# One core, two independent layers in one program: from a hand-written interleaving to a dependency graph with its own static list scheduler

## The chip, the core and the metric

The kernel runs on one core of a Trainium2 chip. The metric is the device time of one execution in microseconds (us), as the median of three runs. The engines, as the profile names them: PE (matrix multiply, with its weight loads shown apart as PEld), DVE and ACT (both can read PSUM, where PE writes), POOL (works on SBUF alone here), and SP, whose queue issues every DMA of this program.

## What is computed

Two layers that share nothing, and whose outputs stand side by side in one array of 2048 x 1152. Layer A is causal attention within four segments of 512 positions plus a memory carried from segment to segment; layer B is a gated long convolution, done as a Fourier transform along time.

```python
# A: x (2048 x 576), 32 heads of 18, 4 segments of 512
for s in range(4):
    qs, ks, vs = q[:, :, s], k[:, :, s], v[:, :, s]
    p = softmax(qs @ ks^T * scale + causal mask)
    a_dot = p @ vs
    a_mem = (phi(qs) @ M) / (phi(qs) @ z + 1e-6)      # phi(t) = t + 1 if t > 0 else exp(t)
    outs.append(g * a_mem + (1 - g) * a_dot)
    M += phi(ks)^T @ vs ; z += sum(phi(ks))
a = concat(outs) @ wo
# B: q, k, v (2048 x 576)
kv = (4-tap shift filter of k) * v
y = irfft(rfft(kv padded to 4096) * rfft(ssm_k padded to 4096))[:2048] + kv * ssm_D
b = q * y
```

## The kernel before

**Layer A** walks 16 iterations i = (segment s, head octet p). Each octet is two groups u of four heads. Per group: `scores` multiplies queries and keys into two-bank PSUM tiles `s` (line 244; 2 buffers, 160 such tiles in all), ACT takes the exponential into `PT` (line 248), POOL zeroes what lies above the diagonal (`_mask`, line 251), and `av` multiplies with V into `po` (line 299), with a second product `pn` against the memory from segment 1 on (line 304). DVE copies `po` and `pn` into `ou`. `norm` collects the denominators by four small DMAs (`cs`), inverts them, sends them through DRAM and back broadcast over partitions (`rb`), and multiplies: the result is `oT`. `out_proj` is the last product, `pout` (line 344), copied to `oA` and stored. Between these stand the projections of the next segment: `pq` (line 169; nine a segment, copied to `q` by DVE and stored to a DRAM scratch that `load_heads` reads back head by head) and `pv` (line 205, copied to `V`). `phik` loads the keys transposed by four DMAs a segment (line 218) for the memory update `pm`.

**Layer B** first makes Fourier tables: POOL writes index patterns, DVE multiplies them (`gw`, lines 457 to 481) and ACT takes the sine. `kv_prep` loads k and v of five channel tiles by transposing DMAs (lines 532, 533), filters on PE (line 551) and stores to DRAM. Then come three groups g of 192 channels: `f1` (line 569, 24 pairs of matmuls for the filter, 24 for kv, copied alternately by ACT and DVE), then 17 steps k1, then six steps of transpose and product (lines 636 and 641, with the copy `Ct` between them on DVE). One step k1 is: two products `f2` on PE (one for the filter, one for kv), copied by DVE as `Hs` (line 616) and by ACT as `X` (line 619); POOL multiplies them into `Y` (line 621); `inverse` on PE (line 595, eight matmuls) takes `Y` of the step before, and ACT copies the result (line 597).

**What sets the order.** Every step is written as a generator; `steps` of A yields 80 times, and after each yield B is advanced in proportion to its count of steps. Tiles come from pools with a fixed number of buffers: 2 for `s`, 4 PSUM banks for all other products, 3 for `PT`, 3 large ones for B, 2 each for `Hs`, `X` and `Y`. Within that, the framework's own scheduler decides the final order on each engine, one instruction at a time, so that a run of matmuls of one product may be split by another's. Copies out of PSUM have a fixed engine: A's on DVE, B's `X` and inverse on ACT, `f1` alternating.

Of the kernel before, what the change touches and what calls it, by code (L numbers as in the profile page):

```python
# [13 lines left out]
I32 = dt.int32  # L14
# [20 lines left out]

VW = H * (DH + 1) + 16
# [6 lines left out]

class Pools:
    def __init__(self, ctx, tc):
        self.ctx, self.tc = ctx, tc
        pool = lambda nm, b, **k: ctx.enter_context(tc.tile_pool(name=nm, bufs=b, **k))
        self.consts = pool("consts", 1)
        self.ps_s = pool("ps_s", 2, space=PSUM)
        self.ps_j = pool("ps_j", 4, space=PSUM)  # L50

        self.x = pool("a_x", 1)
        self.stage = pool("a_stage", 5)
        self.qk = pool("a_qk", 1)
# [4 lines left out]
        self.phik = pool("a_phik", 1)

        self.big = pool("b_big", 3)
        self.io = pool("b_io", 2)
        self.ct = pool("b_ct", 2)
        self.hxy = pool("b_hxy", 2)
        self.dg = pool("b_dg", 1)


class PartA:
    def __init__(self, tc, pl, A_x, A_wq, A_wk, A_wv, A_wo, A_beta, out):
        self.nc = nc = tc.nc  # L70
        self.tc, self.pl = tc, pl
# [3 lines left out]
        consts = pl.consts  # L75
# [6 lines left out]
        def load_w(dst, w, c0, c1):  # L82
            nc.sync.dma_start(out=dst[:, 0:4, :], in_=w[0:512, c0:c1].rearrange("(t p) f -> p t f", p=P))
            nc.sync.dma_start(out=dst[64:128, 4, :], in_=w[512:576, c0:c1])

        self.xs, self.T = {}, {}
        self.load_x(0)
        load_w(self.wqk[:, :, 0:D], A_wq, 0, D)
        load_w(self.wqk[:, :, D:D + 64], A_wk, 512, D)
        load_w(self.wqk[:, :, D + 64:2 * D], A_wk, 0, 512)  # L90
        load_w(self.wv, A_wv, 0, D)

        self.V = [consts.tile([P, 4, VW], BF16, name="V%d" % i) for i in range(2)]
        for v in self.V:
            nc.gpsimd.memset(v[:], 1.0)

        self.qk = [pl.qk.tile([P, 2, 2, L], BF16, name="qk%d" % i) for i in range(2)]
        self.f = [pl.qk.tile([P, 2, L], BF16, name="f%d" % i) for i in range(2)]
        for f in self.f:
            nc.gpsimd.memset(f[:], 0.0)  # L100
        self.Mz_f = consts.tile([P, 8, DH + 1], F32, name="Mz_f")
        nc.vector.memset(self.Mz_f[:], 0.0)
        self.Mz_bd = [consts.tile([P, 8, P], BF16, name="Mz_bd%d" % i) for i in range(2)]
        for m in self.Mz_bd:
            nc.gpsimd.memset(m[:], 0.0)
        self.r_dram = tc.dram_tile([16, 4, 4 * L], BF16, name="a_r_scratch")
        self.qk_dram = [tc.dram_tile([3 * D, L], BF16, name="a_qk_scratch%d" % s) for s in range(NSEG)]

    def late_consts(self):
        nc, consts, A_wo = self.nc, self.pl.consts, self.A_wo  # L110
        self.wo = consts.tile([P, 8, D], BF16, name="wo_sb")
        nc.gpsimd.memset(self.wo[:], 0.0)
        for j in range(4):
            nc.sync.dma_start(out=self.wo[32 * j:32 * j + DH, :, :],
                              in_=A_wo.rearrange("(g j r) f -> j r g f", j=4, r=DH)[j])
# [3 lines left out]
        nc.sync.dma_start(out=bt[:], in_=self.A_beta.partition_broadcast(P))  # L119
        ob = consts.tile([P, H], F32, name="omg")  # L120
        nc.scalar.activation(out=ob[:], in_=bt[:], func=ACT.Exp, scale=1.0)
        nc.vector.tensor_scalar(out=ob[:], in0=ob[:], scalar1=1.0, scalar2=None, op0=ALU.add)
        nc.vector.reciprocal(out=ob[:], in_=ob[:])
        row = consts.tile([P, 1], I32, name="row_a")
        nc.gpsimd.iota(row[:], pattern=[[0, 1]], base=0, channel_multiplier=1)
        ci = consts.tile([P, 8], I32, name="ci_a")
        nc.gpsimd.iota(ci[:], pattern=[[1, 8]], base=0, channel_multiplier=0)

        def bits(sh, mask, nm):
            t = consts.tile([P, 1], I32, name=nm + "_i")  # L130
            nc.vector.tensor_scalar(out=t[:], in0=row[:], scalar1=sh, scalar2=mask,
                                    op0=ALU.arith_shift_right, op1=ALU.bitwise_and)
            f = consts.tile([P, 1], F32, name=nm)
            nc.vector.tensor_copy(out=f[:], in_=t[:])
            return f

        def factors(sh, nm):
            j, u = bits(sh + 1, 3, "j" + nm), bits(sh, 1, "u" + nm)
            nc.vector.scalar_tensor_tensor(out=j[:], in0=u[:], scalar=4.0, in1=j[:], op0=ALU.mult, op1=ALU.add)
            m = consts.tile([P, 4, 8], F32, name="m" + nm)  # L140
            nc.vector.tensor_scalar(out=m[:], in0=ci[:].unsqueeze(1).to_broadcast([P, 4, 8]), scalar1=j[:, 0:1],
                                    scalar2=None, op0=ALU.is_equal)
            nc.vector.tensor_tensor(out=m[:], in0=m[:], in1=ob[:].rearrange("p (a c) -> p a c", c=8), op=ALU.mult)
            g = consts.tile([P, 4], F32, name="g" + nm)
            nc.vector.tensor_reduce(out=g[:], in_=m[:], axis=mybir.AxisListType.X, op=ALU.add)
            return g
        g0, g1 = factors(3, "0"), factors(4, "1")
        kind = bits(3, 1, "kind")
        self.eps = consts.tile([P, 1], F32, name="eps")
        nc.vector.tensor_scalar(out=self.eps[:], in0=kind[:], scalar1=1e-6, scalar2=None, op0=ALU.mult)  # L150
        gt = consts.tile([P, 4], F32, name="gt")
        nc.vector.tensor_scalar(out=gt[:], in0=g1[:], scalar1=-2.0, scalar2=1.0, op0=ALU.mult, op1=ALU.add)
        nc.vector.tensor_scalar(out=gt[:], in0=gt[:], scalar1=kind[:, 0:1], scalar2=None, op0=ALU.mult)
        nc.vector.tensor_tensor(out=g1[:], in0=g1[:], in1=gt[:], op=ALU.add)
        self.gcol = [g0, g1]

    def load_x(self, s):
        xT = self.pl.x.tile([P, 5, L], BF16, tag="xT", name="xT")
        for t in range(5):
            c0 = 128 * t if t < 4 else 448  # L160
            self.nc.sync.dma_start_transpose(out=xT[:, t, :], in_=self.A_x[0, L * s:L * s + L, c0:c0 + P])  # L161
        self.xs[s] = xT


    def proj_qk(self, s, m):
        nc, xT, qd = self.nc, self.xs[s], self.qk_dram[s]
# [533 lines left out]
```

## Time and profile before

| | |
|---|---|
| median of 3 runs | 510.1 us (508.44 to 510.97) |
| the profiled execution's own time | 514.07 us |
| its span, first to last instruction | 512.2 us |
| mean granted PE clock | 0.837 of full |
| PE busy, share of the span | 359.9 us, 70% |
| DVE, ACT, POOL busy | 274.7, 247.7, 191.7 us |

The profiled execution is one run, 1.87 us longer than its span. Busy time is the union of an engine's instructions; waits are idle times of an engine just before an instruction, put down to whichever event came last. No engine is busy throughout, so the question at each place is who waits for whom.

### The profile page before, as it was taken

The page shows a single profiled execution, that of the slowest core. Times are in us where ns is not written, and L with a number is a line of the kernel's source. Part 1 is how long each engine was busy: PE and PEld are TensorE (multiplying, and loading weights), DVE is VectorE, ACT ScalarE, POOL GpSimd, SP SyncE. Part 2 cuts the span into 40 slices and gives each one's busy share as a digit, 9 for nine tenths or more (in the row PEclk, how much of TensorE's full clock was granted, in tenths as well). Part 3 has the DMA queues.
Part 4 walks back from the last instruction along what each step waited for, and adds up shares of the span by engine and source line. Part 5 has one row for each costly group of instructions (what it writes and reads, how often), then busy time and mean ns, then how long its engine had stood idle before and what let it go on. Part 6 is the DMA issues. An engine that isn't in the chain of part 4 may idle for free.

```text
span 512.2 us, 8735 instructions
## 1 busy us (share of the span) xinstructions
PE 359.9 (70%) x3290; PEld 207.4 (40%) x3308; DVE 274.7 (54%) x512; ACT 247.7 (48%) x337; POOL 191.7 (37%) x206
## 2 busy tenths in 40 slices
PE   0924576688868877978857687868868776876535
PEld 0312232243333663644413545636433254654423
DVE  0596285366621945587826744537786324334724
ACT  1078043168736576527747365453657727554100
POOL 9223002032255665302212856732122357663000
PEclk9976598789867899689968879979986679996877
DMA  5541989752414441136254403034444230201031
GB/s 130 159 97 33 195 200 222 172 128 75 112 41 79 122 86 44 53 94 141 79 129 114 112 24 87 26 89 96 116 113 110 77 77 16 64 24 45 12 105 47
DMA packets 100222, 47.96 MB, mean 94 GB/s; under 512 B 80532, under 2 KB 97556, under 8 KB 100180
## 3 DMA queue, kind: packets, MB, share of 16 engines
q1 hardware_dynamic: 100180, 47.41, 37.5%
q8 instruction: 26, 0.43, 0.4%
q14 instruction: 16, 0.13, 0.1%
HBM read 23.72 MB, written 13.80 MB: 73 GB/s over the span
## 4 chain that ended last, share of the span: by engine, by line
PE 40%; DVE 14%; ACT 13%; POOL 11%; DMA 7%; issue 7%; SPq 6%; DVEq 0%; ACTq 0%; POOLq 0%
ACT PT L248 9%; POOL Y L621 9%; PE pq L169 7%; PE pout L344 6%; PE s L244 5%; PE po L299 4%; PE pb L595 4%; SPq L161 3%; PE pb L569 3%; PE pv L205 3%; POOL PT L251 3%; DMA kv<-in_B_k_dram 2%; PE pb L551 2%; DVE Ct L638 2%; PE pb L641 2%
## 5 line engine op out<-in xcount | busy, mean ns | idle before, releaser
L248 ACT ACTIVATE PT<-s 128x1024 bf16<-128x1024 f32 x160 | 156.5, 1030 | 91.5 <-PE po L299 47.2
L251 POOL TENSOR_SCALAR_AFFINE_SELECT PT<-PT 128x512 bf16<-128x512 bf16 (+1 forms) x112 | 78.1, 714 | 226.2 <-ACT PT L248 220.6
L621 POOL TENSOR_TENSOR Y<-X,Hs 128x768 bf16<-128x768 bf16 x51 | 88.4, 1749 | 30.6 <-ACT X L619 23.9
L244 PE MATMUL s<-qk 18*128 18x384 bf16 (+3 forms) x512 | 66.5, 339 | 33.6 <-ACT PT L248 25.6
L169 PE MATMUL pq<-xT,wqk 128*128 128x512 bf16 x165 | 56.9, 460 | 15.2 <-DMA wqk<-in_A_wk_dram 12.6
L595 PE MATMUL pb<-Y,CST 128*128 128x192 bf16 x141 | 29.1, 256 | 43.6 <-POOL Y L621 41.2
L172 DVE CAST q<-pq 128x512 bf16<-128x512 f32 x36 | 24.8, 688 | 59.7 <-PE pq L169 59.4
L244 PEld LDWEIGHTS <-qk 18*128 18x128 bf16 x512 | 19.1, 94 | 75.7 <-issue 63.2
L344 PE MATMUL pout<-wo_sb,oT 128*128 128x288 bf16 x256 | 38.1, 312 | 11.6 <-DVE oT L334 10.4
L616 DVE TENSOR_TENSOR Hs<-pb,DI 128x384 bf16<-128x384 f32 x51 | 28.1, 553 | 33.0 <-PE pb L584 24.7
L301 DVE CAST ou<-po 128x512 bf16<-128x512 f32 x32 | 22.0, 689 | 30.0 <-PE po L299 30.0
L619 ACT CAST X<-pb 128x384 bf16<-128x384 f32 x51 | 24.3, 484 | 25.5 <-PE pb L584 24.7
L344 PEld LDWEIGHTS <-oT 128*128 128x128 bf16 x256 | 26.8, 106 | 21.0 <-DVE oT L334 10.7
L299 PE MATMUL po<-PT,V 128*32 128x128 bf16 (+3 forms) x512 | 32.7, 352 | 3.4 <-issue 1.6
L169 PEld LDWEIGHTS <-wqk 128*128 128x128 bf16 x180 | 19.4, 112 | 38.6 <-issue 14.2
L205 PE MATMUL pv<-wv,xT 128*128 128x288 bf16 x160 | 25.9, 315 | 12.7 <-DVE V L207 10.3
L597 ACT CAST A_kv<-pb 128x384 bf16<-128x384 f32 x45 | 21.8, 483 | 24.9 <-PE pb L595 24.1
L569 PE MATMUL pb<-W1bd,xs 128*128 128x256 bf16 x144 | 27.0, 302 | 4.7 <-DMA xs<-in_B_ssm_k_dram 3.7
L551 PE MATMUL pb<-kv,dg 128*128 128x512 bf16 x77 | 21.4, 420 | 11.1 <-DMA kv<-in_B_k_dram 10.6
L346 DVE CAST oA<-pout 128x288 bf16<-128x288 f32 x32 | 14.4, 454 | 23.2 <-PE pout L344 23.1
L595 PE MATMUL pb<-Y,NSNT 128*128 128x192 bf16 x147 | 26.8, 262 | 0.0
L205 PEld LDWEIGHTS <-xT 128*128 128x128 bf16 x160 | 17.1, 108 | 22.5 <-issue 15.0
(137 smaller groups left out, 592.6 us busy)
## 6 DMA issues: line engine op xcount, KB each, us to landing
rb<-a_r_scratch SPq DMA_DIRECT2D x48, 128.0 KB
qk<-a_qk_scratch SPq DMA_DIRECT2D x128, 36.0 KB
a_qk_scratch<-q SPq DMA_DIRECT2D x32, 128.0 KB
xs<-in_B_ssm_k_dram SPq DMA_DIRECT2D x3, 768.0 KB
xs<-kv_scratch SPq DMA_DIRECT2D x3, 768.0 KB
q_sb<-in_B_q_dram SPq DMA_DIRECT2D x3, 768.0 KB
out_dram<-oA SPq DMA_DIRECT2D x16, 144.0 KB
out_dram<-q_sb SPq DMA_DIRECT2D x3, 768.0 KB
```

The lines of the kernel that those rows point to most:

```text
L169: nc.tensor.matmul(pq[:], lhsT=self.wqk[:, t, 128 * m:128 * m + P], rhs=xT[:, t, :], start=(t == 0), stop=(t == 4))
L205: nc.tensor.matmul(pv[:], lhsT=xT[:, t, P * tt:P * tt + P], rhs=self.wv[:, t, 288 * h:288 * h + 288], start=(t == 0), stop=(t == 4))
L244: self.nc.tensor.matmul(ps[:, b, off:off + n], lhsT=qk[r, 1, u, P * kt:P * kt + P], rhs=qk[r, 0, u, P * kt:L], start=True, stop=True, tile ...
L248: self.nc.scalar.activation(out=dst, in_=ps[:], func=ACT.Exp, scale=self.scale)
L251: self.nc.gpsimd.affine_select(out=ap, in_=ap, compare_op=ALU.is_ge, fill=0.0, base=0, pattern=[[0, n], [1, P]], channel_multiplier=-1)
L299: nc.tensor.matmul(po[32 * j:32 * j + 32, P * kt:L], lhsT=V[:, kt, 19 * h:19 * h + 32], rhs=rhs, start=(kt == 0), stop=(kt == 3), tile_pos ...
L344: nc.tensor.matmul(ps[:], lhsT=oT[:, hg % 2, P * qt:P * qt + P], rhs=self.wo[:, hg, 288 * h:288 * h + 288], start=(hg == 0), stop=(hg == 7))
L551: nc.tensor.matmul(ps[:], lhsT=dg[:, i, :], rhs=t[:, 0, o:o + 512], start=(i == 0), stop=(i == 3))
L569: nc.tensor.matmul(ps[:, u, :], lhsT=xs[:, cc + u, :], rhs=self.W1[:].rearrange("p e k -> p (e k)"), start=True, stop=True)
L595: nc.tensor.matmul(pp[:, o, :], lhsT=tab[:, k1, :], rhs=Y[:, y, :], start=(n == 0), stop=(n == 3))
L616: nc.vector.tensor_tensor(out=Hs[:], in0=ph[:], in1=self.DI[:, g, :, :], op=ALU.add)
L621: nc.gpsimd.tensor_tensor(out=Y[:].rearrange("p (x h) c -> p x h c", x=2), in0=X[:].unsqueeze(2).to_broadcast([P, 2, 2, GB]), in1=Hs[:].un ...
```

## The change

The program keeps its operations, tile sizes and buffer counts, and hands the order to a scheduler in the kernel file. Every step becomes an `op` of a graph, with the tiles and keys it reads and writes, an estimated duration for each engine that may run it, and a priority: rank in program order, from 0 to 1 for A and from 0.03 to 1 for B. `Graph.run` then simulates the engines and emits one op after the other: of all ops whose inputs are scheduled and whose buffers can be had, those of each engine that can start within 0.3 us of its earliest, and of these the one of lowest rank. The framework is told to keep that order (`manual_schedule`). Three more things come with it. Most copies out of PSUM may go to DVE or ACT, wherever they would end first by the estimates. The scratch for q, k and phi(q) is laid out by octets, so that `load_heads` needs 4 DMAs an octet in place of 8 or 12 (64 in all, before 176), while `store_rows` cuts at multiples of 144 rows (91 stores, before 55) and `phik` needs 16 transposes a segment (48 in all, before 12). And the large memsets of A stand ahead of B's tables on POOL.

```diff
+    def run(self):
+        free = {e: 0.0 for e in (PEQ, ACTQ, DVEQ, POOLQ, SPQ)}
...
+                for eng, us, emit in o.alts:
+                    st = max(free[eng], t0)
+                    for d in o.deps:
+                        st = max(st, d.end + d.lat + (0.0 if d.eng == eng and d.lat == 0 else self.SEM))
+                    best.setdefault(eng, []).append((st, o, us, emit, sl))
...
+                m = min(x[0] for x in lst)
+                lst = [x for x in lst if x[0] <= m + 0.3]
+                x = min(lst, key=lambda x: (x[1].prio, x[0]))
...
+def act_us(n):
+    return 0.19 + n / 1200.0
...
+def dve_us(n, rate=1.042):
+    return 0.16 + n * rate * 1e-3
...
+def pe_us(*ns):
+    return sum(max(n / 2400.0, 0.07) + 0.012 for n in ns)
...
+    def copy(self, n, out, in_, r=(), w=(), bf=False):
...
+        return self.G.op([(DVEQ, dve_us(n, 0.53 if bf else 1.042), lambda: nc.vector.tensor_copy(out=out(), in_=in_())),
+                          (ACTQ, act_us(n), lambda: nc.scalar.copy(out=out(), in_=in_()))], r, w)
...
+    def dma(self, kb, fn, r=(), w=(), n=1, transpose=False):
+        us = n * (1.3 if transpose else 0.5)
+        return self.G.op([(SPQ, us, fn)], r, w, lat=2.5 + kb / (60.0 if transpose else 150.0))
...
-        q = self.pl.stage.tile([P, L], BF16, tag="q", name="q")
-        nc.vector.tensor_copy(out=q[:], in_=pq[:])
+        self.copy(L, lambda: q[:], lambda: pq[:], r=[pq], w=[q])
...
         for tt in range(4):
-            nc.sync.dma_start_transpose(out=kt, in_=self.qk_dram[s][D:2 * D, P * tt:P * tt + P])
+            for p in range(4):
+                self.dma(36, lambda tt=tt, p=p: nc.sync.dma_start_transpose(
+                    out=f[:, tt, 144 * p:144 * p + 144], in_=kd[p, 144:288, P * tt:P * tt + P]),
...
-            nc.scalar.copy(out=X[:], in_=px[:])
+            self.copy(2 * GB, lambda X=X: X[:], lambda px=px: px[:], r=[px], w=[X, (A, "x", k1)])
...
+            self.G.op([(POOLQ, 1.75, mul(nc.gpsimd))], r=[X, Hs], w=[Y])
...
+    ctx.enter_context(tc.manual_schedule())
...
-    NB = 10 + NG * (2 * (GB // 8 // 2) + NK1 + 1 + QS // 8)
-    NA = 16 * 5
-    bs, done = b.steps(), 0
-    for i, _ in enumerate(a.steps()):
-        while done < NB * (i + 1) // NA and next(bs, 0) is None:
-            done += 1
+    rank(G.ops[0:n0], 0.0, 0.03)
+    rank(G.ops[n0:n1], 0.0, 1.0)
+    rank(G.ops[n1:], 0.03, 1.0)
+    G.run()
```

The first place is PE in the middle of the 17 steps k1 of the second channel group. Before, the kv product of one step is `pb_3377`, from which `X_3382` and then `Y_3384` are made, and the inverse that needs this `Y` is `pb_3412` (the first matmul of each product is shown, of `pb_3377` the last).

```order
L584 MATMUL pb_3377<-A_kv_2964,CS_169 128x192
...
L595 MATMUL pb_3386<-Y_3362,CST_172 128x192
...
L579 MATMUL pb_3396<-A_h_2614,CS_169 128x192
...
L579 MATMUL pb_3403<-A_kv_2964,CS_169 128x192
...
L595 MATMUL pb_3412<-Y_3384,CST_172 128x192
```

In the changed kernel the kv product is `pp_3344`, from which `X_3363` and `Y_3404` are made, and the inverse that needs it is `pi_3441` (again the last matmul of the first product, and the first of each that follows).

```order
L817 MATMUL pp_3344<-A_kv_2838,CS_77 128x192
...
L832 MATMUL pi_3352<-Y_3318,CST_80 128x192
...
L812 MATMUL pp_3366<-A_h_2559,CS_77 128x192
...
L812 MATMUL pp_3374<-A_kv_2838,CS_77 128x192
...
L812 MATMUL pp_3379<-A_h_2559,CS_77 128x192
...
L812 MATMUL pp_3386<-A_kv_2838,CS_77 128x192
...
L472 MATMUL sc_3392<-qk0_105 128x512
...
L371 MATMUL pq_3416<-xT_3176,wqk_99 128x512
...
L832 MATMUL pi_3429<-Y_3384,CST_80 128x192
...
L832 MATMUL pi_3441<-Y_3404,CST_80 128x192
```

One inverse and two products (16 matmuls) stood between a product and the inverse that needs it; now two inverses, four products, three score tiles and a projection do.

The second place is ACT at the program's start. Before, it holds tables and exponentials only, since DVE makes the copies of `pq` and `pv`.

```order
L121 ACT_TABLE_LOAD
L121 ACTIVATE omg<-beta 128x32
L449 ACT_TABLE_LOAD
L449 ACTIVATE CS<-gw 128x2176
L449 ACTIVATE SN<-gw 128x2176
L449 ACTIVATE psi_f<-psi_i 128x64
L248 ACT_TABLE_LOAD
L248 ACTIVATE PT_450<-s_451 128x1024
```

In the changed kernel all nine copies of `pq` and all eight of `pv` of the first segment stand on ACT, behind the first two sines.

```order
L662 ACT_TABLE_LOAD
L662 ACTIVATE CS<-gw 128x2176
L662 ACTIVATE SN<-gw 128x2176
L245 CAST q<-pq 128x512 x7
L662 ACTIVATE CST<-gw 128x2176
L245 CAST q<-pq 128x512 x2
L245 CAST V_103<-pv 128x16x18 x3
L662 ACTIVATE SNT<-gw 128x2176
L662 ACTIVATE W1bd<-k1pat 128x256
L662 ACTIVATE psi_f<-psi_i 128x64
```

What moved is the work that frees PE's first PSUM banks: from DVE, where it came as it was ready, to ACT, behind the tables.

The third place is SP during the first segment, where the transposed loads of k and v, the keys' transposes `phiK` and the heads of the next octet (`qk`) are issued. Before:

```order
L532 DMA_TRANSPOSE kv<-in_B_k_dram 128x2048
L533 DMA_TRANSPOSE kv<-in_B_v_dram 128x2048
L218 DMA_TRANSPOSE phiK<-a_qk_scratch_140 128x576
L175 DMA a_qk_scratch_141<-q 128x512
L218 DMA_TRANSPOSE phiK<-a_qk_scratch_140 128x576 x3
L557 DMA kv_scratch<-kv 128x2048
L185 DMA a_qk_scratch_141<-e 128x512
L532 DMA_TRANSPOSE kv<-in_B_k_dram 128x2048
L533 DMA_TRANSPOSE kv<-in_B_v_dram 128x2048
L175 DMA a_qk_scratch_141<-q 128x512
L194 DMA qk_126<-a_qk_scratch_140 18x2x512 x8
```

In the changed kernel, from the fourth transpose of `phiK` on:

```order
L429 DMA_TRANSPOSE phiK<-a_qk_scratch_120 128x144
L363 DMA a_qk_scratch_121<-e 128x512
L429 DMA_TRANSPOSE phiK<-a_qk_scratch_120 128x144 x9
L785 DMA kv_scratch<-kv 128x2048
L429 DMA_TRANSPOSE phiK<-a_qk_scratch_120 128x144
L770 DMA_TRANSPOSE kv<-in_B_k_dram 128x2048
L429 DMA_TRANSPOSE phiK<-a_qk_scratch_120 128x144 x2
L770 DMA_TRANSPOSE kv<-in_B_v_dram 128x2048
L363 DMA a_qk_scratch_121<-q 128x512
L402 DMA qk_106<-a_qk_scratch_120 18x4x512 x4
```

The four transposes of `phiK` are now sixteen, and the heads of the next octet (`qk`) stand behind all of them, with 4 loads in place of 8.

## Rows read from the trace of the kernel before

**Rows 1.** The page: span, PE's busy line, and PE's granted clock in 40 slices.
```profile
span 512.2 us, 8735 instructions
PE 359.9 (70%) x3290; PEld 207.4 (40%) x3308; DVE 274.7 (54%) x512; ACT 247.7 (48%) x337; POOL 191.7 (37%) x206
PEclk9976598789867899689968879979986679996877
```
**Rows 2.** Waits: who waited for whom, us in total, times, longest.
```profile
PE pb L595 <- POOL Y L621: 41.2, 29, 3.8
PE s L244 <- ACT PT L248: 25.6, 40, 1.3
PE pb L641 <- DVE Ct L638: 12.8, 13, 3.6
PE pq L169 <- DMA wqk<-in_A_wk_dram: 12.6, 2, 12.2
PE pb L551 <- DMA kv<-in_B_k_dram: 10.6, 3, 7.1
PE pout L344 <- DVE oT L334: 10.4, 1, 10.4
PE pv L205 <- DVE V L207: 10.3, 1, 10.3
PE s L244 <- DMA qk<-a_qk_scratch: 3.9, 5, 2.2
...
SPq L347 <- DVE oA L346: 58.2, 13, 9.9
```
**Rows 3.** Groups by line and form: busy us, mean ns of one, idle before, its releasers.
```profile
L248 ACT ACTIVATE PT<-s 128x1024 bf16<-128x1024 f32 x160 | 156.5, 1030 | 91.5 <-PE po L299 47.2 <-PE s L244 43.0 <-POOL PT L251 0.9
L621 POOL TENSOR_TENSOR Y<-X,Hs 128x768 bf16<-128x768 bf16 x51 | 88.4, 1749 | 30.6 <-ACT X L619 23.9 <-DVE Hs L616 6.4
L619 ACT CAST X<-pb 128x384 bf16<-128x384 f32 x51 | 24.3, 484 | 25.5 <-PE pb L584 24.7 <-POOL Y L621 0.5 <-POOL PT L251 0.2
L638 DVE COPY Ct<-pb 128x1024 bf16<-128x1024 bf16 x18 | 12.4, 686 | 5.6 <-PE pb L636 5.4
L413 ACT CAST A_h<-pb 128x512 bf16<-128x512 f32 x18 | 10.6, 593 | 11.7 <-PE pb L569 11.7
```
**Rows 4.** The chain that ended last, one inverse: start us, us, what.
```profile
170.03 0.82 PE pb L595 x8
```
**Rows 5.** Timeline of the start: start us, us, engine, line, instruction [idle before].
```profile
6.81 1.84 POOL L105 MEMSET Mz_bd<- 128x1024 bf16 x2
10.15 2.01 POOL L464 IOTA fpat<- 128x2176 int32 x1
12.35 3.94 POOL L112 MEMSET wo_sb<- 128x4608 bf16 x1
24.69 2.60 DVE L467 TENSOR_SCALAR gw<-fpat,pcol_f 128x2176 int32<-128x2176 int32 x2
30.46 2.00 ACT L449 ACTIVATE SN<-gw 128x2176 bf16<-128x2176 int32 x1
41.64 4.29 PE L205 MATMUL pv<-wv,xT 128*128 128x288 bf16 x20 [10.31 <-DVE V L207]
```
**Rows 6.** Windows: busy us of the engines, granted clock, DMA share, GB/s.
```profile
45.90:97.50 51.60, 30.79 (x163) 12.11 (x166) 24.67 (x58) 15.85 (x19) 6.66 (x11) 0.82 0.91 201
```
**Rows 7.** Timeline of the end, as rows 5.
```profile
486.43 1.26 PE L299 MATMUL po<-PT,V 128*32 128x512 bf16 x16
...
488.02 3.50 PE L344 MATMUL pout<-wo_sb,oT 128*128 128x288 bf16 x24
...
501.91 7.01 PE L344 MATMUL pout<-wo_sb,oT 128*128 128x288 bf16 x40 [10.39 <-DVE oT L334]
```
**Rows 8.** SP's queue: transposes of one line (ns), and eight loads of heads.
```profile
L218 SPq DMA_TRANSPOSE phiK<-a_qk_scratch x12: 1132/1260/1265, 61.0 to 275.6; - x12
...
74.45 2.90 SPq L194 DMA_DIRECT2D qk<-a_qk_scratch  x8
```

More of the change, by code (lines that the diff above doesn't have):

```diff
@@ L33, in _trig_from_idx, with __init__, __getitem__, slot @@
     nc.scalar.activation(out=out_bf, in_=tmp2[:], func=ACT.Sin, bias=math.pi, scale=-2.0 * math.pi / modulus)
+PEQ, ACTQ, DVEQ, POOLQ, SPQ = "PE", "ACT", "DVE", "POOL", "SP"
+class Slots:
+    def __init__(self, pool, tag, bufs, fifo=True):
+        self.pool, self.tag, self.fifo = pool, tag, fifo
+        self.slots = [None] * bufs
+        self.made, self.given = 0, 0
+class Tl:
+    def __init__(self, ring, shape, dtype, name):
+        self.ring, self.shape, self.dtype, self.name = ring, shape, dtype, name
+        self.left, self.end, self.tile = 0, 0.0, None
+        self.no = ring.made
+        ring.made += 1
+    def __getitem__(self, k):
+        return self.tile[k]
+    def slot(self):
+        r = self.ring
+        if r.fifo and r.given != self.no:
+            return None
+        best = None
+        for i, o in enumerate(r.slots):
+            if o is None:
+                return i, 0.0
+            if o.left == 0 and (best is None or o.end < best[1]):
+                best = i, o.end
+        return best
+    def give(self, i):
+        r = self.ring
+        r.given += 1
+        r.slots[i] = self
+        self.tile = r.pool.tile(self.shape, self.dtype, tag="%s%d" % (r.tag, i), name=self.name)
@@ L59, in __init__ @@
[L59 to L71, printed above, removed]
+        pool = lambda nm, **k: ctx.enter_context(tc.tile_pool(name=nm, bufs=1, **k))
+        self.consts = pool("consts")
+        self.sb = pool("work")
@@ new lines, in __init__ @@
+        self.Mz_bd = [consts.tile([P, 8, P], BF16, name="Mz_bd%d" % i) for i in range(2)]
+        self.wo = consts.tile([P, 8, D], BF16, name="wo_sb")
+        nc.gpsimd.memset(self.V[0][:], 1.0)
+        for q in self.qk:
+            nc.gpsimd.memset(q[:, 4:6, :], 0.0)
+        nc.gpsimd.memset(self.V[1][:], 1.0)
+        nc.vector.memset(self.Mz_f[:], 0.0)
+        for m in self.Mz_bd:
+            nc.gpsimd.memset(m[:], 0.0)
+        nc.gpsimd.memset(self.wo[:], 0.0)
+        self.r_dram = tc.dram_tile([16, 4, 4 * L], BF16, name="a_r_scratch")
@@ L86, in __init__ @@
+        self.qk_dram = [tc.dram_tile([4, 432, L], BF16, name="a_qk_scratch%d" % s) for s in range(NSEG)]
         self.xs, self.T = {}, {}
         self.load_x(0)
[L88 to L95, printed above, removed]
@@ L646, in group, with tr @@
-        nc.sync.dma_start(out=self.o_view[:, :, D + ch0:D + ch0 + GB], in_=q[:])
-    def steps(self):
-        yield from self.kv_prep()
-        for g in range(NG):
-            yield from self.group(g)
+            pt = self.psj([P, 8, P], "pt", BF16)
+            def tr(qq=qq, pt=pt):
+                cf = A[:]
+                for u in range(8):
+                    in_ap = bass.AP(cf.tensor, cf.offset + (qq + u), [[cf.ap[0][0], P], [QS, P]])
+                    nc.tensor.transpose(out=pt[:, u, :], in_=in_ap, identity=self.ident[:])
@@ new lines, in group @@
+            self.pe(8 * 0.085, tr, r=[(A, "c", k1) for k1 in range(NK1)] + ["ident"], w=[pt])
+            Ct = Tl(pl.ct, [P, 8, P], BF16, "Ct")
+            self.copy(1024, lambda Ct=Ct: Ct[:], lambda pt=pt: pt[:], r=[pt], w=[Ct], bf=True)
+            py = self.psj([P, 8, 64], "py")
+            self.pe(8 * 0.085, lambda Ct=Ct, py=py: [nc.tensor.matmul(
+                py[:, u, :], lhsT=Ct[:, u, :], rhs=self.Psi[:].rearrange("p e t -> p (e t)"), start=True, stop=True)
+                for u in range(8)], r=[Ct, "Psi"], w=[py])
```

869 lines of the change are left out of this document (511 added, 358 removed).

## The prediction

> **What bounds the kernel now.** First the page: PE is busy 359.9 of 512.2 us, more than any other engine, and idle 152.3 [rows 1]. Its work is needed whatever the order, so what the change can win is that idle time, and what PE's clock gives back when it idles less. The granted clock has two levels, 1.2 and 2.4 GHz, and averages 0.837 of full, so a third of the time (0.163 / 0.5 = 0.326) was spent at the low one.
>
> Then PE's waits. Seven rows carry 123.5 us of the 152.3: 41.2 for `Y` from POOL, 25.6 for score tiles that ACT has not yet read, 12.8 for the copy `Ct`, 12.6 for the first weights, 10.6 for transposed k, 10.4 for the last `oT`, 10.3 for copies of V [rows 2]. The other 28.8 us are small. These are not waits for a saturated engine: POOL, the slowest in a step k1, is busy 37% of the span, ACT 48%, DVE 54% [rows 1]. PE comes too early to the one instruction that stands next in its fixed order. So the question for each wait is how much PE work the new order puts between a producer's start and its user.
>
> **The change, wait by wait** (PE idle before, then after).
>
> *`Y`: 41.2 to 4.* From the end of a kv product to the inverse that needs it lie the copy X (0.48), the multiplication (1.75) and three handovers of about 0.1: 2.5 us [rows 3]. In the order before, what PE has in between is one inverse and two products, 16 matmuls at 0.10 us, as eight take 0.82 [rows 4]: 1.66 us. Counting this over the whole order, each matmul priced by its kind and all scaled to PE's 359.9 us, 33 of the 51 steps have less than 2.5 us of cover before, and one after; the place shown has 5.6 us. A mask ahead of `Y` on POOL lengthens some, and I leave 4.
>
> *Scores: 25.6 to 6.* A score tile can be written again when its exponential, 1.03 us [rows 3], has read it. Of 158 pairs of tiles that share a buffer, 45 have under 1.2 us of PE work between them before, and 13 after.
>
> *`Ct`: 12.8 to 3.* The copy takes 0.69 us [rows 3], 0.85 with its handovers. All 18 have less cover before, one after.
>
> *First weights: 12.6 to 11.5.* The weights are now issued ahead of the five transposes of x; those still have to land, so little is won.
>
> *V copies: 10.3 to 5.* DVE held them behind the tables; now ACT takes all copies of `pq` and `pv`, behind the first two sines. That makes a new wait: on POOL `fpat` now stands behind the memset of `wo_sb`, so it ends at 8.65 + 3.94 + 0.6 for three small ones + 2.01 = 15.2 us, four table operations on DVE at 1.30 end at 20.4, the sine SN at 22.4, and the first copy at 23. PE has filled its four PSUM banks by about 18, with four products of some 1.5 us from 11.5 on [rows 5]. Five us of waiting there; V's own copies then follow as PE produces them.
>
> *Transposed k: 10.6 to 5.* The first kv load stood behind x of the next segment; now it stands ahead, behind the sine CST. The rest of this stretch stays bound by transfers: DMA share 0.91 at 201 GB/s from 45.9 to 97.5 us [rows 6]. So B's start is won, not the whole stage.
>
> *The end: 10.4 to 12.* From the last `po` at 486.4 to the first matmul with the last `oT` at 501.9 lies a chain of DMAs and DVE that the change leaves. Before, 24 of the last 64 output matmuls (3.5 us) stood in that gap, since they could be split from their groups; a graph op is never split, so all 64 now follow, and instead about 2.3 us of B's last steps cover the gap [rows 7].
>
> Sum of idle: 4 + 6 + 3 + 11.5 + 5 + 5 + 12 = 46.5, and the 28.8 us of small waits kept: 75.3.
>
> *New waits: 23 (0 to 104).* By the order, 101 copies that DVE made now stand on ACT (28 of q, 24 of V, 20 of `oA`, 18 of `po`, 11 of `pn`), where each may find an exponential running, and 60 copies of ACT's (31 X, 29 others) on DVE. If each of the 101 cost PE a whole exponential, 104 us [rows 3]. The copy itself is no dearer: 0.59 us on ACT for 512 columns [rows 3]. Exponentials take 165 us, 0.37 of the forecast's span, and a copy that meets one waits half of 1.03: 0.19 us on average, 19 in all, if PE stood on each. I take 19 and 4 for the copies on DVE. The sums of busy time allow it: ACT goes from 248 to about 268, DVE from 275 to about 251.
>
> *PE's busy time: -12 (0 to -58).* A third of 359.9 at the low clock is 117 us that would be 58 shorter at the high one [rows 1]. PE's idle share falls from 30% to some 22%, so I take a fifth of that.
>
> *DMA: 0 (0 to 45).* SP issues 36 more transposes and 36 more stores, and 112 fewer loads of heads. A load costs 0.36 us of the queue (8 in 2.90), a transpose 1.26 at 576 rows; at 144 rows there is no row, and I take the same: +45, +13 to 20, -40 us [rows 8]. What hides the rest is that SP itself waits, 58 us on `oA` alone [rows 2]. Without that cover the sixteen transposes ahead of a segment's second octet cost 12 x 1.26 = 15 us in each of three segments. The Trainium skill ("DMA: Bandwidth & Descriptors", Rules for kernel authors) says to coalesce small transfers, since under 64 KB one pays mostly overhead; a quarter transpose moves 36 KB and the new pieces of a store 16 KB and up, so by that rule these two edits are wrong, and the kernel ends at the SP rival's time below, while the merged heads are right. No row of before shows a quarter transpose.
>
> **Sum.** 359.9 - 12 + 75.3 + 23 = 446.2 us of span. The profiled execution was 1.87 us longer than its span: 448.1. The runs' median stands to that execution as 510.1 to 514.07, so 448.1 x 0.9923 = 444.6, say 445.
>
> **Rivals.**
>
> *SP's queue bounds the segments* (489): the sixteen transposes and the cut stores push head loads back, 15 us in each of three segments. For it: everything is issued by one queue in a fixed order, planned with PE times that are too short (five 512-column matmuls are planned at 1.13 us). Against it: PE has all of the next segment's projections to do meanwhile, and before, PE waits on heads 3.9 us in all [rows 2]. 446.2 + 45 + 1.9 = 493.1, x 0.9923 = 489.
>
> *Slower: copies behind exponentials* (537). The four PSUM banks that all products share fill up behind ACT, which is held by runs of two to four exponentials. If each of the 101 copies costs PE 1.03 us and the clock gives nothing: 359.9 + 75.3 + 104 + 1.9 = 541, x 0.9923 = 537. It decides for slower from 80 us of such waits, four in five. For it: ACT now holds all early copies of q and V. Against it: before, B's copies already stood on ACT among exponentials, and no row of PE names one.
>
> *The order does not carry over* (511, no change): the planned order assumes durations that do not hold, and `Y`, scores and `Ct` wait as before: 79.6 in place of 13, +66.6 us, 514.7 x 0.9923 = 511. Against it: the planned 1.75 and 1.04 are the rows' 1749 and 1030 ns [rows 3], and a PE slower than planned makes cover longer.
>
> *Better* (405): no new waits and half of the clock's 58: 359.9 - 29 + 75.3 + 1.9 = 408, x 0.9923 = 405.
>
> **Chances.** Forecast 0.62 (425 to 465 by itself), SP 0.14, better 0.11, no change 0.06, slower 0.07. The range leaves out slower, no change and over half of better, 0.20: 420 to 492. Faster by over 0.5%, about what a measurement of this kernel can tell from no change: 0.62 + 0.14 + 0.11 = 0.87; within: 0.06; slower: 0.07.
>
> **What would show it.** In the waits after, PE's row for `Y` under 10 us and those for scores and `Ct` under 10 each; a PE wait of some 5 us on copies of q near 20 us; PE's products of V done by 40 us, where before they only started again at 41.6 [rows 5]; PE busy 80% or more between 100 us and the last `po`, the mean clock over 0.85; all 64 last output matmuls behind the last `oT`. I am wrong if PE waits for copies on ACT or DVE by tens of us, if SP's loads of heads end PE's waits, or if `Y` still does.

## The result, and the profile after

The changed kernel takes 426.6 us (median of four executions, 419.0 to 432.4); the kernel before took 509.8 beside it. The ratio is 0.827, 95% interval 0.818 to 0.836. The forecast was 445, with a range of 420 to 492. Two of the four executions, the profiled one among them, ran at a lower clock (0.883 and 0.863, against 0.907 and 0.902), so the ratio rests on the other two (423.9 and 419.0), and what one kernel gains or loses against another is taken below from the ratios, times 510 us. By its ratio the change wins 88 us.

The page: span, busy time of the engines, and PE's granted clock in 40 slices, to set beside [rows 1].

```profile
span 427.5 us, 8667 instructions
PE 338.2 (79%) x3286; PEld 198.0 (46%) x3308; DVE 270.0 (63%) x476; ACT 261.5 (61%) x370; POOL 197.4 (46%) x206
PEclk9976898965987999956998998995998999999958
```

The span fell by 84.7 us. PE's idle time fell by 63.0 (152.3 to 89.3), and PE's busy time, for the same matmuls, by 21.7. The mean granted clock rose from 0.837 to 0.883. PE's longest waits, to set beside [rows 2] (us in total, times, longest):

```profile
PE pout L581 <- DVE oT L570: 11.0, 2, 8.9
PE pq L371 <- ACT q L245: 8.4, 1, 8.4
PE pq L371 <- DMA xT<-in_A_x_dram: 7.6, 4, 5.8
PE sc L472 <- ACT PT L475: 6.7, 11, 1.4
PE sc L472 <- DMA qk<-a_qk_scratch: 5.8, 5, 2.6
...
PE pc L778 <- ACT A_h L245: 3.5, 1, 3.5
PE pv L411 <- ACT q L245: 3.0, 2, 2.3
...
PE py L887 <- DVE Ct L244: 2.3, 5, 0.8
PE pi L832 <- POOL Y L866: 2.1, 4, 1.0
```

`Y`, scores and `Ct`, which cost 79.6 us before, now cost 11.1. To see which stage this came from, the run is cut at 40 us, at 100 us and at the last `po`. Windows of the kernel before, then of the changed one (start and end, length, PE busy and its matmuls, granted clock, DMA share, GB/s):

```profile
0.00:40.00 40.00, 15.80 (x69) 0.89 0.49 124
40.00:100.00 60.00, 37.36 (x200) 0.78 0.79 175
100.00:486.40 386.40, 294.60 (x2940) 0.84 0.31 79
486.40:512.20 25.80, 12.13 (x83) 0.75 0.26 76
```

```profile
0.00:40.00 40.00, 20.58 (x72) 0.84 0.69 144
40.00:100.00 60.00, 42.59 (x240) 0.84 0.63 147
100.00:398.30 298.30, 261.76 (x2865) 0.91 0.42 105
398.30:427.50 29.20, 13.27 (x114) 0.74 0.25 72
```

The long middle stage fell from 386.4 to 298.3 us. Of these 88.1 us, 55.3 are idle time (91.8 to 36.5). The other 32.8 are busy time: 10.0 moved ahead of 100 us (63.2 in place of 53.2), 1.1 moved behind the last `po`, and the other 21.7 went at a clock of 0.91 in place of 0.84. The end grew by 3.4 us. The stretch from 40 to 100 us is still poor: PE is idle for 17.4 of 60.

### The profile page after: what moved, and what is told of

Read it like the earlier page. It is cut to its first block, busy times and chain, and to the rows that moved or that the text cites. A ratio compares the mean times of both kernels' runs of the same rounds, so it can differ in the third digit from the quotient of the medians.

```text
span 427.5 us, 8667 instructions
## 1 busy us (share of the span) xinstructions
PE 338.2 (79%) x3286; PEld 198.0 (46%) x3308; DVE 270.0 (63%) x476; ACT 261.5 (61%) x370; POOL 197.4 (46%) x206
## 4 chain that ended last, share of the span: by engine, by line
PE 40%; DVE 17%; SPq 12%; DMA 11%; issue 7%; ACT 6%; POOL 5%; DVEq 0%; ACTq 0%; POOLq 0%
PE pout L581 6%; PE sc L472 6%; PE pi L832 5%; SPq L429 4%; PE pc L778 4%; PE pq L371 3%; DMA cs<-ou 3%; PE po L519 2%; PE pf L800 2%; SPq L363 2%; PE pv L411 2%; ACT PT L475 2%; DMA qk<-a_qk_scratch 2%; POOL Y L866 2%; SPq L542 2%
## 5 line engine op out<-in xcount | busy, mean ns | idle before, releaser
L475 ACT ACTIVATE PT<-sc 128x1024 bf16<-128x1024 f32 x160 | 157.0, 1032 | 33.8 <-PE sc L472 25.9
L472 PE MATMUL sc<-qk 18*128 18x384 bf16 (+3 forms) x512 | 63.2, 328 | 16.0 <-ACT PT L475 6.7
L858 DVE TENSOR_TENSOR Hs<-pp,DI 128x384 bf16<-128x384 f32 x51 | 27.9, 551 | 12.0 <-POOL Y L866 5.8
L832 PE MATMUL pi<-Y,CST 128*128 128x192 bf16 x141 | 28.2, 256 | 4.9 <-POOL Y L866 2.1
L800 PE MATMUL pf<-W1bd,xs 128*128 128x256 bf16 x144 | 25.2, 293 | 5.1 <-DVE A_kv L244 2.9
L519 PE MATMUL po<-PT,V 128*32 128x256 bf16 (+3 forms) x512 | 25.8, 323 | 4.4 <-DVE kv L781 3.7
L245 ACT CAST q<-pq 128x512 bf16<-128x512 f32 x28 | 16.0, 592 | 20.3 <-DMA a_qk_scratch<-q 11.1
L778 PE MATMUL pc<-kv,dg 128*128 128x512 bf16 x77 | 24.0, 461 | 5.2 <-ACT A_h L245 3.5
L832 PE MATMUL pi<-Y,NSNT 128*128 128x192 bf16 x147 | 25.4, 255 | 0.0
L244 DVE CAST A_kv<-pi 128x384 bf16<-128x384 f32 (+1 forms) x30 | 15.8, 528 | 12.0 <-PE pi L832 11.6
```

Source lines behind the costliest of these rows:

```text
L472: nc.tensor.matmul(ps[:, b, off:off + n], lhsT=qk[r, 2 + u, P * kt:P * kt + P], rhs=qk[r, u, P * kt:L], start=True, stop=True, tile_positi ...
L475: self.act(act_us(1024), lambda: nc.scalar.activation(out=dst(), in_=ps[:], func=ACT.Exp, scale=self.scale), r=[ps], w=[key])
L519: nc.tensor.matmul(po[32 * j:32 * j + 32, P * kt:L], lhsT=V[:, kt, 19 * h:19 * h + 32], rhs=rhs, start=(kt == 0), stop=(kt == 3), tile_pos ...
L778: self.pe(pe_us(*[512] * 4), lambda c=c, t=t, dg=dg, ps=ps: [nc.tensor.matmul(ps[:], lhsT=dg[:, i, :], rhs=t[:, 0, KPAD + 512 * c - i:KPAD ...
L800: self.G.op([(PEQ, pe_us(256, 256), lambda cc=cc, ps=ps: [nc.tensor.matmul(ps[:, u, :], lhsT=xs[:, cc + u, :], rhs=self.W1[:].rearrange("p ...
L832: nc.tensor.matmul(pp[:, o, :], lhsT=tab[:, k1, :], rhs=Y[:, y, :], start=(n == 0), stop=(n == 3))
```

## The experiments

Theory: the gain is an order planned with about the right durations, which puts work between a producer and its user; the clock then follows. Rivals: the split of copies over two engines makes it; any fine mixing of the two layers makes it; and, for what the change costs, SP's queue.

| kernel | median, us | ratio to before, 95% |
|---|---|---|
| the changed kernel | 426.6 | 0.827 (0.818 to 0.836) |
| copies on fixed engines | 437.2 | 0.852 (0.847 to 0.858) |
| order by rank | 700.3 | 1.370 (1.365 to 1.374) |
| order by rank, framework's scheduler | 532.3 | 1.042 (1.038 to 1.046) |
| planned, framework's scheduler | 507.9, again 502.9 | 0.977 (0.969 to 0.985) |
| two false durations in the plan | 468.5 | 0.915 (0.909 to 0.922) |
| quarter transposes of `phiK` later | 432.8 | 0.845 (0.838 to 0.851) |
| whole transposes of `phiK` | 404.2 | 0.791 (0.788 to 0.793) |
| whole, and memsets behind the table | 401.4 | 0.785 (0.780 to 0.790) |
| whole, and A's ranks to 0.96 | **395.8** | 0.772 (0.766 to 0.778) |
| all three | 405.3 | 0.793 (0.787 to 0.799) |
| whole, 0.96, PE priced 1.1 times | 403.4 | 0.788 (0.782 to 0.795) |

**Copies on fixed engines.** `f1` alternates by `on=ACTQ if cc // 2 % 2 == 0 else DVEQ`.

```diff
-    def copy(self, n, out, in_, r=(), w=(), bf=False):
+    def copy(self, n, out, in_, r=(), w=(), bf=False, on=DVEQ):
...
+        return self.G.op([a for a in alts if a[0] == on], r, w)
...
-                      lambda px=px: px[:], r=[px], w=[X, (A, "x", k1)])
+                      lambda px=px: px[:], r=[px], w=[X, (A, "x", k1)], on=ACTQ)
```

> Edit: each copy out of PSUM has the one engine that it had before the change (q, V, ou, oA and Ct on DVE, X and the inverses on ACT, pf alternating); scheduler, layout and everything else stay. By the theory that the gain is the planned order: the order is planned anew around the fixed engines, and counted over it the covers stay (no k1 step with less than 2.4 us of PE work between its kv product and its inverse, 14 of 158 score pairs under 1.2 us), so Y, score and Ct waits of PE stay under 10 us each and the time is 427, at most 8 away. By the rival that the gain is the split of copies by load: the copies of po, q and pout wait on DVE again, and the time goes to 450 or more, with PE waits for copies on DVE of 20 us and more.

437.2 us: by the ratios 13 us above the changed kernel, more than the 8 that the theory allowed and well short of the rival's 450. `Y` ends no wait of PE in it, and scores and `Ct` wait little:

```profile
PE pq L372 <- DVE q L244: 9.9, 3, 7.8
PE sc L473 <- ACT PT L476: 7.3, 17, 1.1
PE py L889 <- DVE Ct L244: 3.5, 6, 1.4
```

The wait that the rival named did come, though: all of PE's waits that end with a copy on DVE add up to 43 us here, and 5 more end with one on ACT; in the changed kernel copies on either engine end 31. So the covers hold without the split, and the split is worth some 13 us of the 88.

**Order by rank alone**, and, as a second kernel, the same without the line `ctx.enter_context(tc.manual_schedule())`, so that the framework's scheduler orders again.

```diff
             for eng, lst in best.items():
-                m = min(x[0] for x in lst)
-                lst = [x for x in lst if x[0] <= m + 0.3]
                 x = min(lst, key=lambda x: (x[1].prio, x[0]))
-                if pick is None or x[0] + x[2] * 0.0 < pick[0][0]:
+                if pick is None or x[1].prio < pick[0][1].prio:
```

> Edit: the scheduler no longer looks at planned times for the order; of all operations whose inputs are scheduled and whose buffers are free, it emits the one of lowest rank (program order of A and B, merged by rank). Copies still go to whichever engine would end first, and the layout stays. By the theory of the planned order: counted over this order, 48 of 158 score pairs have under 1.2 us of cover (13 in the changed kernel, 45 before it), 11 of 18 Ct copies under 0.85 (1 and 18), but only 6 of 51 Y under 2.5 (1 and 33). At the waits that such counts had before the change (25.6 us for scores, 12.8 for Ct, 41.2 for Y) this gives scores 27, Ct 8 and Y 6 to 8, together 30 us over the changed kernel, and transfers that now stand in program order on SP add to it: 460, between 450 and 500. By the rival that split copies and merged head loads make the gain: within 2% of 427.

> Edit: as the kernel in program order by rank, and in addition the framework's own scheduler decides the final order on each engine again, as in the kernel before the change. What is left of the change is the layout of the scratch, the split of copies and the fine merging of A and B by rank. Counted over the order: 51 score pairs under 1.2 us, 7 of 18 Ct under 0.85, 11 of 51 Y under 2.5 us, short by 11.8 us in all. Theory of the planned order: Y 15 to 19 us, scores 28, Ct 5, together some 38 over the changed kernel: 465, between 450 and 485. Rival, split and layout make the gain: within 2% of 427.

700.3 and 532.3 us, both far beyond the theory's numbers and in its direction; so split, layout and fine merging without a planned order are slower than the kernel before. The 700 tell less about covers than about a fixed order: whatever has the lowest rank blocks its engine until its input has come. PE's waits in the first of the two:

```profile
PE pi L830 <- POOL Y L864: 65.5, 14, 10.0
PE pc L776 <- DVE dg L771: 38.0, 3, 13.2
PE pf L798 <- DMA xs<-in_B_ssm_k_dram: 36.1, 3, 18.5
PE sc L470 <- ACT PT L473: 32.5, 50, 1.8
```

The scores wait somewhat more than the count said (27 expected). `Y` waits up to 10 us, which a count of PE's work cannot give: something ahead of `Y` in a fixed order on DVE, ACT or POOL was late; which of them is open. In the second kernel scores wait 33.0 us and `Y` 12.2, near their counts, but transposed k costs another 29.5, and PE is busy 390.6 us at a clock of 0.81: the theory's number left out both.

**Planned, but the framework orders.** The changed kernel without one line; buffers, copy engines and layout are as planned. It was run twice, for a second profile.

```diff
-    ctx.enter_context(tc.manual_schedule())
```

> Edit: the changed kernel without the line that tells the framework to keep the order. The planner still emits its order and gives out the buffers and engines, but the framework's scheduler decides again what each engine does next. Counted over the order that results: 46 of 158 score pairs under 1.2 us of cover (13 in the changed kernel, 45 before it), 6 of 51 Y under 2.5 us (1 and 33), 1 of 18 Ct under 0.85 us. Theory that the covers pay: scores wait 25 to 30 us, Y 5 to 8, together some 25 to 30 over the changed kernel: 453, between 443 and 470. Rival, that line matters little once buffers and engines are planned: within 2% of 427.

> The kernel of the run without manual_schedule once more, for a second profile: its first profiled execution had a clock of 0.683, while the other nine executions had 0.81 to 0.84 at 497 to 510 us. Theory that PE's waits make its loss against the changed kernel: at a clock near 0.82 PE is busy 345 to 360 us and idle 145 to 160, of which the covers that were counted (scores 25 to 33, Y 5 to 10) explain some 25 to 30 more than in the changed kernel, and the other 30 to 40 are waits for copies and transfers that the framework's order moves. Rival, the clock makes it: PE busy near 400 us again and idle near 115.

507.9 and 502.9 us: without this line, 77 of the 88 us are lost by the ratios. I had expected 25 to 30. This is the cleanest test of the order: the operations and the layout are the same, and of each kind of copy as many stand on each engine (28 of the 36 of q on ACT in both, for one). The second profile has PE busy 372.0 us at a clock of 0.818, and idle for 133.8. Its waits:

```profile
PE sc L472 <- ACT PT L475: 28.6, 43, 2.9
PE pv L411 <- ACT q L245: 12.6, 2, 6.8
PE pp L812 <- DVE A_kv L244: 12.0, 3, 10.9
PE pf L800 <- DMA xs<-kv_scratch: 10.8, 1, 10.8
PE pq L371 <- ACT V L245: 9.9, 1, 9.9
```

Against the changed kernel that is 44.5 us more of idle time and 33.8 more of busy time. The scores are 21.9 of the idle time, as counted. The other four rows add some 42 us, more than the rest, while other waits shrank (that of `pq` for copies of q from 8.4 to 1.9). The planner had put each copy where it would end first, and the new order may undo that; this is not shown. Neither of the two explanations holds alone: idle time makes somewhat over half of the difference, and busy time at the lower clock the rest.

**Two false durations.** The planned order is kept, but an exponential and `Y` are planned too short.

```diff
-        self.act(act_us(1024), lambda: nc.scalar.activation(out=dst(), in_=ps[:], func=ACT.Exp, scale=self.scale),
+        self.act(0.2, lambda: nc.scalar.activation(out=dst(), in_=ps[:], func=ACT.Exp, scale=self.scale),
...
-            self.G.op([(POOLQ, 1.75, mul(nc.gpsimd))], r=[X, Hs], w=[Y])
+            self.G.op([(POOLQ, 0.1, mul(nc.gpsimd))], r=[X, Hs], w=[Y])
```

> Edit: the changed kernel, with two numbers of the planner alone made false: an exponential of a score tile is planned at 0.2 us (its row has 1032 ns) and the multiplication into Y at 0.1 us (its row has 1723 ns). Nothing that is executed changes but the order. Theory that the gain is an order planned with the right durations: 39 of 158 score pairs have under 1.2 us of PE work between them (13 in the changed kernel, 45 before it), and 15 of 51 k1 steps under 2.5 us between the kv product and the inverse (1 and 33), short by 7.4 us in all; at the waits that such counts had before, scores wait 22 us and Y 12, some 25 over the changed kernel: 452, between 440 and 465. Rival, any fine mixing of the two layers does it, the durations don't matter: within 2% of 427.

468.5 us, by the ratios 45 over the changed kernel and above the theory's range. The two waits are back, and no other has grown by as much:

```profile
PE 348.6 (75%) x3308; PEld 204.9 (44%) x3308; DVE 230.8 (50%) x401; ACT 293.2 (63%) x445; POOL 193.2 (42%) x206
...
PE sc L472 <- ACT PT L475: 29.3, 56, 1.4
PE pi L832 <- POOL Y L866: 24.3, 22, 2.8
```

They are 44.8 us longer than in the changed kernel; between the two profiles PE's idle time grew by 25.9 in all, since other waits shrank, and its busy time by 10.4. The operations and the way of choosing are the same, and two numbers make half of the gain, so fine mixing alone does not do it. But more than the order changed: with exponentials planned so short, 75 more instructions went to ACT (445 in place of 370) and as many fewer to DVE, all of them copies. PE's waits that end with a copy did not grow by it (21 us, and 31 in the changed kernel), yet copies ahead of an exponential on ACT can make a score tile wait longer, and the trace does not part that from the order. The counts foresaw 34 us of such waits and gave `Y` half of what it cost.

**`phiK` later, and `phiK` whole.** The first only moves the quarter transposes in rank; the second makes them whole again, from a second copy of the keys (a store of each tile more).

```diff
+                self.late.append(o)
...
+    for o in a.late:
+        o.prio += 0.05
```

```diff
+        if kind == 1 and s < NSEG - 1:
+            self.dma(n, lambda: nc.sync.dma_start(out=self.k_dram[s][f0:f0 + n, :], in_=tile[r0:r0 + n, :]),
+                     r=[key], w=[("kd", s, f0 // 128)])
...
+            self.dma(144, lambda tt=tt: nc.sync.dma_start_transpose(
+                out=f[:, tt, 0:D], in_=kd[:, P * tt:P * tt + P]),
```

> Edit: the changed kernel with its 48 quarter transposes of phiK, whose rank alone is made 0.05 later, so that SP issues the heads of the next octet and the loads of k and v of layer B ahead of most of them. Theory that what they cost is their place in SP's queue: heads and kv loads come 10 to 15 us earlier in the first segment, and most of what whole transposes won (23 us) is won here as well: 404 to 414. Rival, their number costs (36 more issues of 1.23 us, and 36 more transfers in small pieces), wherever they stand: 420 to 432, as the changed kernel.

> Edit: the keys of segments 0 to 2 are stored a second time, in a scratch of 576 rows, and phiK is loaded from it by four transposes of 576 rows a segment in place of sixteen of 144 (36 fewer in all), with 15 more stores. In the changed kernel a quarter transpose took 1.23 us of SP's queue, as long as a whole one before, and from 55 to 90 us SP does nothing but issue one transfer after the other, while PE is busy only 7.9 of the 16 us from 80 to 96. Theory that SP's queue costs there: SP gets 12 x 1.23 less 5 x 0.45 = 12.5 us back a segment, the loads of heads at 90.2 us come 10 us earlier, and most of PE's idle time from 84 to 95 us goes: 418 (411 to 423). Rival, the later two segments and this hole are bound by something else (transfers under way, or copies): within 1% of the changed kernel.

Later: 432.8 us, nothing won and by the ratios 9 us lost. Whole: 404.2, by the ratios 18 us won, twice what was expected. So what they cost is their number and not their place. In the changed kernel SP's queue during the first segment (start us, us, instruction) is one issue after the other:

```profile
58.63 3.79 SPq L429 DMA_TRANSPOSE phiK<-a_qk_scratch  x3
...
68.43 12.22 SPq L429 DMA_TRANSPOSE phiK<-a_qk_scratch  x9
...
84.89 2.51 SPq L429 DMA_TRANSPOSE phiK<-a_qk_scratch  x2
87.44 2.10 SPq L770 DMA_TRANSPOSE kv<-in_B_v_dram  x1
89.59 0.58 SPq L363 DMA_DIRECT2D a_qk_scratch<-q  x1
90.21 1.48 SPq L402 DMA_DIRECT2D qk<-a_qk_scratch  x4
```

The price per issue in the changed kernel, and the window of the nine in a row:

```profile
L429 SPq DMA_TRANSPOSE phiK<-a_qk_scratch x48: 1101/1232/2272, 58.6 to 277.2; - x48
...
68.40:80.70 12.30, 9.27 (x58) 0.86 0.15 37
```

A quarter takes 1.23 us of the queue, a whole one 1.26 [rows 8]. While SP issued the nine, the DMA engines were busy at a share of 0.15 and moved 37 GB/s: the queue was the limit, not the transfers. With whole transposes the same four stretches read:

```profile
0.00:40.00 40.00, 21.73 (x81) 0.87 0.71 151
40.00:100.00 60.00, 49.32 (x414) 0.87 0.83 193
100.00:376.10 276.10, 246.90 (x2704) 0.94 0.44 109
376.10:406.10 30.00, 13.56 (x113) 0.70 0.22 65
```

Here the heads that SP issued at 90.2 us in the changed kernel go out earlier:

```profile
73.35 1.60 SPq L406 DMA_DIRECT2D qk<-a_qk_scratch  x4
```

PE is busy 6.7 us more between 40 and 100 us, at a DMA share of 0.83, and the middle stage is 22.2 us shorter. Of the 21.4 us between the two spans 14.7 are idle time, 6.7 of it between 40 and 100 us and 7.3 in the middle stage; the rest is busy time. That SP's queue is the cause was followed for the first segment only; for the later ones it is not shown. In the kernel with later transposes the hole has only moved, to 100 us, where SP issues six of them ahead of heads and PE waits for the heads (SP, then PE):

```profile
97.78 7.50 SPq L429 DMA_TRANSPOSE phiK<-a_qk_scratch  x6
...
107.27 1.44 SPq L402 DMA_DIRECT2D qk<-a_qk_scratch  x4
...
109.94 1.50 PE L473 MATMUL sc<-qk 18*128 18x256 bf16 x6 [6.07 <-DMA qk<-a_qk_scratch]
```

**The start and the end**, each on top of whole transposes. For the start, the memsets of V, qk and `Mz_bd` are changed as that of `wo_sb`.

```diff
-        nc.gpsimd.memset(self.wo[:], 0.0)
+        self.pool(3.95, lambda: nc.gpsimd.memset(self.wo[:], 0.0), w=[("wo", j) for j in range(4)])
```

```diff
-    rank(G.ops[n0:n1], 0.0, 1.0)
+    rank(G.ops[n0:n1], 0.0, 0.96)
```

> Edit: the kernel with whole transposes of phiK (404.2), and the memsets of V, qk, wo_sb and Mz_bd become operations of the graph, so that they stand behind the iota fpat on POOL instead of ahead of it. In its base fpat ends at 15.2 us, the second sine at 23.6, and PE waits 7.2 us for the first copy of q until 24.1. Theory that POOL's memsets set this wait: fpat ends near 6.7 us, the second sine near 15, the first copies of q follow by 16, and the start is won in full: 397 (394 to 400), with under 2 us of waiting for copies of q. Rival, the start of the segment is bound by the transfers behind it (x, weights, k and v): PE's wait goes but comes back as waits for transfers, and the time stays within 3 us of 404.

> Edit: the kernel with whole transposes of phiK (404.2), and the ranks of layer A end at 0.96 instead of 1. So the last octet of A is ahead of B's last steps: behind the last po stand 12 matmuls of the inverse and all six steps of transpose and product, where its base has two. In the base PE waits 10.8 us for the last oT. Theory that this wait is only a chain of transfers with too little work beside it: the added work, some 6 us of PE, goes into the gap, and the time falls to 398 (395 to 401). Rival: DVE, which makes the copies Ct and the products with q in B's last steps, holds up the chain of the last oT (inverting and multiplying on DVE), or the earlier order loses as much elsewhere: 402 to 408.

The start: 401.4 us, 3 won by the ratios, whose intervals overlap: the rival's number. PE's wait for q is gone, but the planner then issues loads of k and v ahead of the first heads, and PE waits for those:

```profile
46.19 0.39 PE L475 MATMUL sc<-qk 18*128 18x256 bf16 x1 [6.87 <-DMA qk<-a_qk_scratch]
```

The end: 395.8 us, 10 won by the ratios, as the theory said. PE's wait for the last `oT`, in the base and then here:

```profile
PE pout L584 <- DVE oT L573: 11.8, 2, 10.8
```

```profile
PE pout L584 <- DVE oT L573: 1.9, 1, 1.9
```

**All three, and a dearer PE.** The latter is the former without the memsets, and with `return 1.1 * sum(...)` in `pe_us`.

> Edit: whole transposes of phiK, the ranks of A that end at 0.96, and the large memsets behind the first table on POOL, all three. Theory that the three act in different stretches and add up: 395.8 less the 2.8 that the memsets won by themselves, 393 (389 to 396). Rival, the memsets' gain was within what the order varies by, since every edit makes the planner choose a new order: 394 to 400.

> Edit: the kernel with whole transposes and ranks of A that end at 0.96 (395.8), with the planner's prices of PE's operations times 1.1, since PE is planned to be busy 304 us and is busy 336 in that kernel's profile. Theory that the order pays by having the right durations: covers are already there (2 to 5 score pairs under 1.2 us in both, 2 and 3 Y under 2.5), so little is left to win: 394 (390 to 398). Rival, the planner's too fast PE places transfers wrongly, and waits for heads and x go (15 us in that kernel): 385 to 390.

405.3 and 403.4 us: by the ratios 11 and 9 us slower than the kernel with A's ranks to 0.96, where neither theory nor rival reached that far up. In the kernel of all three PE waits 10.1 us for heads, in its base 6.0, and 5.3 us for one copy of `oA`. An edit of the plan changes the whole order, and I take it that this by itself moved the time by as much as these edits were to win; no run parts the two. The same doubt lies on the 10 us of the end, though there the wait that was aimed at went, and on a part of the 18 of the whole transposes. 395.8 us is the best of the kernels here.

## Why the prediction was right, and where it was off

**The mechanism held.** PE's waits were a matter of a fixed order in which PE came too early, and the planned order covered them. Foreseen for `Y`, scores and `Ct`: 4, 6 and 3; measured: 2.1, 6.7 and 2.3. PE busy from 100 us to the last `po`: 88% (over 80 foreseen). That the order makes most of it, and not the split, is shown by the missing line (77 us lost at the same split) against the fixed engines (13 lost); the false durations (45 lost) say that the durations matter.

**DMA: 0 was wrong, and some 18 us were there.** This is the step that failed: I took SP's queue as hidden, because SP itself waited 58 us on `oA` [rows 2]. But in the kernel before, the first copy into `oA` starts at 216.2 us (ns each, then first and last start), so none of that cover lay in the first segment, where issues already filled 42 of the 45 us from 46 to 91:

```profile
L346 DVE CAST oA<-pout x32: 395/457/459, 216.2 to 509.0; 128x288 bf16<-128x288 f32 x32
```

The rival of SP's queue had the right mechanism, the right price per issue (1.26 taken, 1.23 measured) and the wrong reach: 45 us over three segments, where the whole transposes won 18. The Trainium skill's rule against small transfers ("DMA: Bandwidth & Descriptors", Rules for kernel authors), which spoke against this edit, holds here in its direction, with the numbers above: a quarter transpose takes as long to issue as a whole one. The time of 489 that the prediction tied to it did not come. The cut stores, of which it says the same, were not tried apart.

**PE's busy time: -12 was too little.** It fell by 21.7: of the 58 us that the low clock cost, more than a third came back, where I gave it a fifth. So it is in part luck that the sum came near: this term and the waits paid for the DMA term. Without that cost the kernel takes 404.2, about the 405 of the rival *Better*, to which I gave 0.11.

**Waits at the start.** First weights and x: 11.5 foreseen, 7.6 measured. PE so ran out of PSUM banks earlier, at 15.5 in place of 18 us (8.4 us of waiting that ended at 23.9), while the first copy came when foreseen. ACT at the start:

```profile
21.36 2.02 ACT L662 ACTIVATE SN<-gw 128x2176 bf16<-128x2176 int32 x1 [0.57 <-DVE gw L670]
23.29 2.03 ACT L245 CAST q<-pq 128x512 bf16<-128x512 f32 x4
```

So the new wait was 8.4 us, not 5, and products of V stood 3.0 more behind copies of q; they were done at 42.9 us, not by 40. Transposed k: 5 foreseen, no wait in the trace.

**The end**: 12 foreseen, 11.0 measured, but by another way. I had all 64 output matmuls behind the last `oT`; 58 were, since a matmul of a group waits only for the `oT` that it reads itself. The covering work of B was there.

```profile
398.33 0.73 PE L519 MATMUL po<-PT,V 128*32 128x512 bf16 x16
...
413.96 9.90 PE L581 MATMUL pout<-wo_sb,oT 128*128 128x288 bf16 x58 [8.86 <-DVE oT L570]
```

**New waits.** What is left of the 89.3 us after the six waits above that the sum named (38.1) and 3.0 for copies of q is 48.2, where I had 51.8 (28.8 and 23). This rest holds both PE's waits for copies and what SP's queue cost as idle time, and the trace does not part them: in the hole PE's largest wait carries the name of a copy (`pc <- A_h`, 3.5), and that for heads is 5.8 us in all. By the names alone, copies on ACT and DVE end 31 us of PE's waits; 14 of them (8.4 and 3.0 for q, 2.3 for `Ct`) are counted above, and 17 stand against the 23 that I took. So the term is about right as a sum; how it splits is open.

## What to carry to other kernels

When PE idles for engines that are themselves half idle, plan the whole order against measured durations and have it kept: here a false duration for two kinds of operation cost half of the gain, and a second scheduler behind the plan most of it. Price every issue on the one queue that issues DMAs, stretch by stretch, at its own duration and not by its bytes; a queue that waits somewhere in the run is not free where it is full. And once an order is planned, expect a small edit to move the time by several us through the new order alone, so that gains of 1 to 2% need a repeat with another order.

## What the runs showed of the hardware

PE's busy time for the same matmuls ran from 324.9 us at a mean clock of 0.919 (whole transposes, 0.96, dearer PE) over 338.2 at 0.883 (the changed kernel) and 372.0 at 0.818 (planned, framework's scheduler) to 400.0 at 0.735 (order by rank). In these four PE was idle for 76.7, 89.3, 133.8 and 298.7 us. So less idle time came with less busy time: from the third to the second, 44.5 us of idle time went with 33.8 of busy time. It is no fixed rate, though: from the kernel before to the changed one, 63.0 went with 21.7, and the third kernel idled less than the kernel before (133.8 and 152.3) at no higher clock (0.818 and 0.837). What holds better is the product: busy time times the mean clock is 294 to 304 us in these four and 301 in the kernel before (316 in the order by rank under the framework's scheduler).

The issue of a transposing DMA took SP the same time for 144 rows as for 576 (median 1.23 and 1.26 us); one of 2048 rows took 2.10. The Trainium skill says that spreading DMAs over the issuing engines gives no bandwidth but saves issue time ("DMA: Bandwidth & Descriptors", Rules for kernel authors); by the share of 0.15 it is issue time that was short here. No run tried it, nor whether transposes may be issued from two engines at a time.
